# Sliding-window attention feeding a routed MLP: half-width values, in-place keys, 64-row score tiles, chained loads

## The chip, the cores and the metric

The kernel runs on one core of a Trainium2 chip. The time is the device time of one execution in microseconds. The kernel before took 681.13 us (median of 3 runs, 680.95 to 684.59). The profiled execution took 682.57 us; its span from first to last instruction is 680.8 us, at a mean granted TensorE clock of 0.992.

Names of engines: PE is TensorE (PEld its weight loads), DVE is VectorE, ACT is ScalarE, POOL is GpSimd, SP is the sync engine, which here only starts transfers.

## The reference

```python
# attention: 8 batches, 8 heads, 512 local and 32 global rows, head_dim 64
out_g = softmax(q_g @ [k_g, k_l].T / 8) @ [v_g, v_l]           # global rows see everything
s_ll  = where(abs(i - j) <= 32, q_l @ k_l.T / 8, -1e9)         # local rows: a band of +-32
out_l = softmax([q_l @ k_g.T / 8, s_ll]) @ [v_g, v_l]          # ... and the 32 global keys
x     = concat([out_g, out_l], rows), heads side by side       # (8, 544, 512)
# routing: logits = x @ w_gate (8 experts); local = sigmoid(x @ w_local)
# the expert of a row is the argmax of its logits, or the row before's if local >= 0.5
out   = softmax(logits)[e] * (relu(x @ w1[e]) @ w2[e])         # 512 -> 1024 -> 512, fp32
```

## The kernel before, in words

Two stages follow each other. **Attention** fills the first 228 us or so; the routed MLP ("MoE") fills the rest. The change lies in attention and in the hand-over of buffers to the MoE.

*Tiling of attention.* Two heads make a pair, so a batch has four pairs; a pair's 64 + 64 head dimensions fill the 128 partitions. The 512 local rows are 16 windows of 32 rows. A window needs 128 keys: its own 32, the 32 on each side, and the 32 global ones; so its scores are one 128-wide block.

- `load` and `loadv` start a pair's transfers on the SP queue: q and k into a `raw` buffer (528 KB, four buffers) and v into a `v` buffer (1040 KB, four buffers). v comes from memory already arranged as the 128 value rows of every one of the 16 windows, so each value row is stored about twice and the global ones 16 times.
- `prep` (GpSimd) builds from `raw` what the scores read: `qbd`, a block-diagonal q (head 0's 64 dimensions in partitions 0 to 63, head 1's below, zeros elsewhere, written once by `blank`), and `kx`, the keys with the global 32 between the local ones, so that any window's 128 keys are contiguous. `cp` does this with GpSimd's affine_select.
- `l_m` writes the band mask into two PSUM banks with a matmul of the identity. `l_s` adds the scores: one matmul a window with 128 contraction rows, 64 output columns (2 heads by 32 queries) and 128 keys; two windows stand side by side in a bank.
- `l_max` (DVE) takes the row maximum and subtracts it, `l_exp` (ACT) exponentiates, `l_t` (PE, then ACT) transposes, `l_av` multiplies by v: 128 rows, 32 columns, 65 wide (a column of ones gives the sum); then DVE divides into `xa`, the batch's rows.
- The global queries of two pairs make a unit "g" (`g_s`, `g_max`, `g_exp`, `g_t`, `g_av`), which reads k in `raw` and six of the 16 window arrangements of v (`GCH`).

*Order.* Everything is written out by hand in `run`: 48 steps, of a batch l0, l1, g0, l2, g1, l3 (l = a pair, g = the global queries of two). Step s does scores, maximum and exponent of unit s and transposes and values of unit s - 2. Engines execute their queues in the order in which `run` writes them. In between stand pieces of later work: `fpiece(wide)` and `fpiece(thin)` (f1 transposes finished rows, f2 and f3 compute gate logits), and `drip`, which puts one or a few small DVE or GpSimd instructions of the routing (`gens`) between others. `moe.pre` starts, in the last four steps, the first gathers of MoE rows (`gather`, GpSimd), the first weight loads, and splits of weights into high and low parts (`split`, `flush`; two of them with the subtraction on GpSimd). `f4` stores a finished batch's rows: one transfer of 1056 KB on the ACT queue (SP for the last two batches) and small ones for the global rows.

*PSUM.* Scores of l and g units and some routing pieces share three banks (`ps0` to `ps2`); a unit takes two, so a unit's second bank is one that the unit before last, or the one before, must have released: DVE's subtraction releases a bank.

Lines of the profile: L246 scores, L235 mask, L263 transposes of l units, L279 values, L331/L342 the same of g units, L299 global scores, L355 f1, L370 f2, L190 GpSimd copies, L251/L253 maximum and subtraction, L282 to L287 division, L307 maximum of g units, L1284/L1296 the MoE's matmuls, L1191 the low part of weights, L1224 gathers.

## Time and profile before

| | busy us of 680.8 | in 123.00 to 149.20 (one batch in the middle of attention) |
|---|---|---|
| PE | 651.2 | 25.84 |
| PEld | 560.6 | 21.31 |
| DVE | 430.1 | 21.31 |
| ACT | 344.6 | 16.07 |
| POOL | 205.8 | 11.03 |
| DMA engines, mean share | | 0.86 (299 GB/s) |
| profiled execution / its span | 682.57 / 680.8 us | |
| median of the runs | 681.13 us | |

A batch repeats every 26.2 to 26.3 us there. Busy time of PE counts matmuls as pipelined, with modelled ends; rows of one line that overlap the next line's are shown with their own length, while the chain of waits shows what each adds.

### The profile page before, as it was taken

What the parts mean: (1) busy time and instruction counts of PE and PEld (TensorE: products, weight loads), DVE (VectorE), ACT (ScalarE), POOL (GpSimd) and SP (SyncE); (2) the same over time, 40 slices, a digit from 0 to 9 for tenths busy, and PEclk for the clock granted to TensorE, in tenths of its full rate; (3) what the DMA queues carried; (4) which work ended last, traced back from release to release, by engine and by line L of the source; (5) the groups of instructions that cost most, each with busy time, mean ns of one, the idle gap of its engine ahead of it and who ended that gap; (6) DMA issues with size and microseconds to landing.
All of it is one profiled execution on the core that took longest, in us unless ns stands there. A gap on an engine that the chain in (4) does not pass through costs nothing.

```text
span 680.8 us, 18547 instructions
## 1 busy us (share of the span) xinstructions
PE 651.2 (96%) x7261; PEld 560.6 (82%) x7261; DVE 430.1 (63%) x1090; ACT 344.6 (51%) x620; POOL 205.8 (30%) x342
## 2 busy tenths in 40 slices
PE   8899999998999999999999999999999999999994
PEld 6688788786776879887889888889898989898893
DVE  7878687787987877976407545526363627265552
ACT  4465665664555764555317626334455326166543
POOL 7644344343662310033012313040304020133113
PEclk9999999999999999989999999999999999999997
DMA  8857978879585596867318566437374626175583
GB/s 321 350 202 265 322 253 333 306 260 345 206 317 201 194 344 214 294 199 235 117 41 293 201 252 201 148 101 272 88 274 139 218 67 243 54 277 185 182 288 99
DMA packets 43013, 151.46 MB, mean 222 GB/s; under 512 B 7965, under 2 KB 9245, under 8 KB 38688
## 3 DMA queue, kind: packets, MB, share of 16 engines
q1 hardware_dynamic: 32080, 120.42, 50.5%
q0 software_dynamic: 6960, 21.90, 9.8%
q10 hardware_dynamic: 3744, 6.63, 2.6%
q8 instruction: 78, 1.28, 0.8%
q14 instruction: 151, 1.24, 0.6%
HBM read 130.55 MB, written 19.69 MB: 221 GB/s over the span
## 4 chain that ended last, share of the span: by engine, by line
PE 81%; DVE 10%; issue 4%; POOL 2%; ACT 1%; DMA 1%; POOLq 0%; ACTq 0%; DVEq 0%
PE ps L1284 27%; PE ps L1296 23%; PE ps L246 7%; PE ps L263 4%; PE ps L279 4%; PE ps L1238 3%; PE ps L1301 2%; PE ps L355 2%; DVE wp L1191 2%; PE ps L342 2%; PE ps L299 2%; PE ps L331 2%; PE ps L370 1%; DVE pe L253 1%; DVE mx L251 1%
## 5 line engine op out<-in xcount | busy, mean ns | idle before, releaser
L1312 POOL DMA_INDIRECT out_dram<-y,tk x39 | 41.3, 1058 | 311.8 <-ACT y L1309 155.4
L1284 PE MATMUL ps<-wp,wp 128*128 128x256 f32 (+6 forms) x744 | 118.0, 318 | 0.0
L1284 PEld LDWEIGHTS ps<-wp,wp 128*128 128x128 f32 x744 | 112.0, 189 | 5.4 <-ACT wp L1240 0.4
L1296 PE MATMUL ps<-wp,wq 128*128 128x512 f32 x444 | 111.5, 398 | 0.5 <-DVE wq L1288 0.5
L1296 PEld LDWEIGHTS ps<-wp,wq 128*128 128x128 f32 x444 | 81.6, 188 | 17.8 <-ACT wq L1286 0.7
L1288 DVE SCALAR_TENSOR_TENSOR wq<-ps,wq 128x384 fp32r<-128x384 f32 (+4 forms) x120 | 44.9, 409 | 55.9 <-ACT wq L1286 49.8
L1286 ACT ACTIVATE wq<-ps 128x256 fp32r<-128x256 f32 (+6 forms) x88 | 39.4, 452 | 72.7 <-PE ps L1284 65.8
L190 POOL TENSOR_SCALAR_AFFINE_SELECT qbd<-raw 64x512 f32<-64x512 f32 x62 | 44.3, 715 | 97.3 <-PE ps L246 89.0
L1241 DVE TENSOR_TENSOR wp<-ps,wp 128x512 fp32r<-128x512 f32 x40 | 27.6, 691 | 71.5 <-ACT wp L1240 71.3
L246 PE MATMUL ps<-kx,qbd 128*64 128x128 f32 x1024 | 64.7, 276 | 3.7 <-issue 3.6
L246 PEld LDWEIGHTS ps<-kx,qbd 128*64 128x64 f32 x1024 | 55.4, 137 | 11.7 <-issue 9.1
L251 DVE TENSOR_REDUCE mx<-ps 128x4 f32<-128x512 f32 x64 | 43.8, 685 | 30.0 <-PE ps L246 28.8
L1309 ACT ACTIVATE y<-ps,pp 128x512 f32<-128x512 f32 x39 | 26.8, 687 | 66.4 <-PE ps L1296 60.2
L257 ACT ACTIVATE pe<-pe 128x512 f32<-128x512 f32 x64 | 40.8, 638 | 37.9 <-DVE pe L253 37.9
L1191 DVE TENSOR_TENSOR wp<-raw,wp 128x1024 fp32r<-128x1024 f32 x47 | 56.7, 1218 | 4.5 <-ACT wp L1178 4.3
L1224 POOL DMA_INDIRECT xa<-xs,idx x42 | 50.5, 1203 | 17.3 <-issue 11.1
L1240 ACT CAST wp<-ps 128x512 fp32r<-128x512 f32 x40 | 23.3, 586 | 55.5 <-PE ps L1238 55.5
L1178 ACT CAST wp<-raw 128x1024 fp32r<-128x1024 f32 x49 | 50.6, 1047 | 0.9 <-PE ps L342 0.6
L253 DVE TENSOR_TENSOR pe<-ps,mx 128x512 f32<-128x512 f32 x64 | 43.9, 686 | 1.0
L190 POOL TENSOR_SCALAR_AFFINE_SELECT kx<-raw 128x384 f32<-128x384 f32 (+3 forms) x127 | 42.8, 370 | 2.7 <-DMA raw<-in_qk_dram 0.6
L279 PEld LDWEIGHTS ps<-v,pt 128*32 128x32 f32 x2048 | 32.1, 110 | 11.4 <-issue 8.8
L265 ACT COPY pt<-ps 128x512 f32<-128x512 f32 x64 | 34.7, 599 | 10.8 <-PE ps L263 10.8
(284 smaller groups left out, 1183.0 us busy)
## 6 DMA issues: line engine op xcount, KB each, us to landing
raw<-in_w_dram SPq DMA_DIRECT2D x78, 512.0 KB
v<-in_vw_dram SPq DMA_DIRECT2D x32, 1040.0 KB
raw<-in_qk_dram SPq DMA_DIRECT2D x32, 528.0 KB
xa<-in_w_dram SPq DMA_DIRECT2D x26, 512.0 KB
xT<-in_w_dram SPq DMA_DIRECT2D x20, 512.0 KB
xs<-xa ACTq DMA_DIRECT2D x6, 1056.0 KB
xs<-xa SPq DMA_DIRECT2D x2, 1056.0 KB
qgb<-in_qg_dram SPq DMA_DIRECT2D x8, 128.0 KB
```

The source lines that it names most:

```text
L190: self.nc.gpsimd.affine_select(out=out, in_=in_, pattern=pat, compare_op=ALU.is_ge, fill=0.0, base=0, channel_multiplier=0)
L246: nc.tensor.matmul(sp[64 * t2:64 * t2 + 64, t], qbd[:, w], kf[:, f:f + P], start=False, stop=True, skip_group_check=True)
L251: nc.vector.tensor_reduce(out=mx, in_=st["sps"][hb], axis=AX.X, op=ALU.max)
L253: nc.vector.tensor_tensor(out=st["pe"][:, 4 * hb:4 * hb + 4], in0=st["sps"][hb], in1=mx.broadcast_to([P, 4, P]), op=ALU.subtract)
L279: nc.tensor.matmul(o[32 * w4:32 * w4 + 32, g, h], pt[:, 2 * g + w4 // 2, w4 % 2, h, :], v[:, w, h * (D + 1):(h + 1) * (D + 1)], start=True ...
L1178: (nc.vector.tensor_copy if dve else nc.scalar.copy)(out=hi, in_=raw)
L1191: (nc.gpsimd if pool else nc.vector).tensor_tensor(out=lo[:, f], in0=raw[:, f], in1=hi[:, f].bitcast(F32), op=ALU.subtract)
L1224: self.nc.gpsimd.indirect_dma_start(out=self.xr[j] if k == "early" else self.xr4[:, j], out_offset=None, in_=src, in_offset=bass.IndirectO ...
L1284: nc.tensor.matmul(ph, a[:, dc, fs], b_[:, dc, n0:n1], start=(n == 0), stop=(n == 11))
L1288: nc.vector.scalar_tensor_tensor(out=t, in0=ph[:, a - n0:b_ - n0], scalar=0.0, in1=hh[:, fc, a:b_].bitcast(F32), op0=ALU.max, op1=ALU.subt ...
L1296: nc.tensor.matmul(py, a[:, fc, js], b_[:, fs], start=(fc == 0 and k == 0), stop=(fc == 7 and k == 2))
L1312: sc = nc.gpsimd.indirect_dma_start(out=self.out, out_offset=bass.IndirectOffsetOnAxis(ap=self.g[1][:, j:j + 1], axis=0), in_=y, in_offset ...
```

## The change

1. **v by halves.** Only the 128 value rows of the eight even windows are loaded (520 KB a pair). `prepv` lets GpSimd build the odd windows' rows in a second tile `w` (three buffers): one copy of 96 partitions by 1040 elements and one of 32 partitions by 910 that moves from partitions 0-31 to 96-127. The even windows read `v`, the odd ones `w`.
2. **Keys in place.** `kx` is gone. `raw` is 2064 wide instead of 1056; the loaded keys stand in pairs of 64 in the order `PO`, and `prep` writes, with two copies of 448 elements, 14 blocks of 64 (global keys, a neighbour's keys) behind them in the same buffer. A window's 128 keys are now two blocks of 64 at two places (`keys`).
3. **Narrow scores.** Pairs 0 and 2 of each batch (`NARROW`) have no `qbd`: `l_sn` issues 32 matmuls of 64 contraction rows by 32 columns, one for each window and head, head 0 into one bank and head 1 into the other; then come both maxima. Pairs 1 and 3 keep `l_s`. The mask is written by two matmuls a bank, each half as wide, in place of one.
4. **Chain of loads.** `get` makes each q/k or v load, from the fourth, wait until the last but one load before it has landed.
5. **Row stores.** A batch's rows leave as two halves on the SP queue, at most one half a step; the small store `gx` goes to SP too.
6. **Order.** `fpiece(thin)` (f2, f3) moves from ahead of the exponent to between the two `l_av` (or behind `g_av`); `g_exp` has three activations in place of five, with the global scores split at 320 instead of 256; `blank` and the mask stand differently at the start.
7. **Space.** The gathered rows `xr`, the MoE's output tiles `y` and one weight buffer now lie in the wider `raw` buffers.

```diff
-GCH = [1, 4, 7, 10, 13, 14]
+GCH = [8, 2, 11, 5, 14, 0]
+PO = [0, 2, 3, 5, 6, 1, 4, 7]
+AHEAD, FREE = 2, 3
+NARROW = (0, 2)
...
+    def get(self, out, in_):
+        d = self.nc.sync.dma_start(out, in_)
+        if len(self.sent) >= FREE:
+            self.tc.add_manual_dep(d.ins, self.sent[-AHEAD].ins.name, ..., reason="chain")
+        self.sent.append(d)
...
+        if not u["n"]:
+            qbd = u["qbd"] = self.qbd()
             self.cp(qbd[0:64, :, 0, :], q[0:64], [[0, NW], [0, 32]])
             self.cp(qbd[64:128, :, 1, :], q[64:128], [[0, NW], [0, 32]])
-        self.cp(kf[:, 1:5]...); self.cp(kf[:, 6:24]...); self.cp(kf[:, 24]...); self.cp(kx[:, 1:8, 2, :]...)
+            self.cp(x[:, :, 0], g, [[0, 14], [0, 32]])
+            self.cp(x[:, :, 1], k[:, 1:15], [[0, 14], [0, 32]])
...
+    def prepv(self, u):
+        w = self.w()
+        self.cur[b]["v"][pr] = (v, w)
+        self.cp(w[0:96], v[0:96], [[0, 8], [0, VW]])
+        self.cp(w[96:128, 0:7], v[0:32, 1:8], [[0, 7], [0, VW]])
...
+    def l_sn(self, st):
+        for t2 in range(2):
+            for par in range(2):
+                for w4 in range(4):
+                    m = 4 * t2 + w4
+                    w = 2 * m + par
+                    k = self.keys(st, m, par)
+                    for h in range(2):
+                        d = slice(64 * h, 64 * h + 64)
+                        nc.tensor.matmul(st["sps"][h][32 * w4:32 * w4 + 32, 2 * par + t2],
+                                         st["qk"][d, 32 * w:32 * w + 32], k[d], start=False, stop=True, ...)
...
                 if npr < len(pairs):
                     self.prep(pairs[npr])
+                self.prepv(nx)
+            self.store(1)
...
-            if nl:
+            if nl and nx["n"]:
+                self.l_sn(nx)
+                self.l_max(nx, 0)
+                self.l_max(nx, 1)
+            elif nl:
                 self.l_s(nx, 0)
                 self.l_max(nx, 0)
...
-            fpiece(thin)
             if nl:
                 self.l_exp(nx, 0)
             ...
             if sl:
                 self.l_av(st, 0)
+                fpiece(thin)
                 self.l_av(st, 1)
...
-        self.xr = [buf.tile([P, ROW], F32, name=f"xr{j}") for j in range(2)]
+        self.xr = [raw.t[j][:, 1024:1024 + ROW] for j in range(2)]
```

How the rows move is shown at three places.

On PE, in step l2 of the first batch, before (L235 writes the mask, L246 the scores, L279 the values):

```order
L263 MATMUL ps_68<-idf,pe_138 128x128 x4
L235 LDWEIGHTS idb
L235 MATMUL ps_63<-mask,idb 128x4x2x32
L235 LDWEIGHTS idb
L235 MATMUL ps_64<-mask,idb 128x4x2x32
L246 MATMUL ps_63<-kx_146,qbd_144 64x128 x8
L246 MATMUL ps_64<-kx_146,qbd_144 64x128 x8
L279 MATMUL ps_70<-v_134,pt_142 32x65 x16
```

and the same place after (L258 mask, L284 the narrow scores, of which the first three of 32 are shown):

```order
L302 MATMUL ps_68<-idf,pe_139 128x128 x4
L258 LDWEIGHTS idb
L258 MATMUL ps_63<-maskn,idb 128x4x32
L258 LDWEIGHTS idb
L258 MATMUL ps_63<-maskn,idb 128x2x2x32
L258 LDWEIGHTS idb
L258 MATMUL ps_64<-maskn,idb 128x4x32
L258 LDWEIGHTS idb
L258 MATMUL ps_64<-maskn,idb 128x2x2x32
L284 MATMUL ps_63<-raw_79 32x128
L284 MATMUL ps_64<-raw_79 32x128
L284 MATMUL ps_63<-raw_79 32x128
```

Sixteen matmuls of 64 columns, eight for one bank and then eight for the other, became 32 of 32 columns that alternate between the banks; the mask has four matmuls and weight loads in place of two.

On DVE, at the start of the program, from the mask to the first row maximum, before:

```order
L146 CAST mask<-m_155 128x512
L147 MEMSET mask 64x32
L148 MEMSET mask 64x32
L202 COPY qbd_144<-raw_77 64x16x32
L203 COPY kx_146<-raw_77 128x7x32
L217 MEMSET qbd_145 64x16x32
L218 MEMSET qbd_145 64x16x32
L219 MEMSET kx_147 128x32
L220 MEMSET kx_147 128x64
L455 MEMSET pg_149 128x768
L251 TENSOR_REDUCE mx_119<-ps_63 128x4
```

and after (`maskn` is the narrow pairs' mask; L157 waits for two GpSimd copies that read it):

```order
L153 CAST maskn<-m_155 128x2x32 x2
L154 CAST maskn<-m_155 128x128
L157 MEMSET maskn 32x32
L158 MEMSET maskn 32x32
L159 MEMSET mask 64x32
L160 MEMSET mask 64x32
L225 COPY raw_77<-raw_77 128x14x32
L500 MEMSET pg_148 128x768
L241 MEMSET qbd_145 64x16x32
L242 MEMSET qbd_145 64x16x32
L241 MEMSET qbd_146 64x16x32
L242 MEMSET qbd_146 64x16x32
```

All four large `qbd` memsets now stand between the first pair's keys and the first maximum; before, two of them stood there and two ahead of the mask.

On POOL, at the end of attention (L1224 and L1191 before, L1280 and L1247 after, are the MoE's first gathers and splits), before:

```order
L1224 DMA xr_86<-xs,idx 128x528
L1224 DMA xr_87<-xs,idx 128x528
L190 AFFINE_SELECT qbd_145<-raw_80 64x16x32 x2
L190 AFFINE_SELECT kx_147<-raw_80 128x128
L190 AFFINE_SELECT kx_147<-raw_80 128x6x64
L190 AFFINE_SELECT kx_147<-raw_80 128x32
L190 AFFINE_SELECT kx_147<-raw_80 128x7x32
L1224 DMA xr_86<-xs,idx 128x528
L1224 DMA xr_87<-xs,idx 128x528
L1191 TENSOR_TENSOR wp_100<-raw_77,wp_100 128x256 x4
L1191 TENSOR_TENSOR wp_101<-raw_78,wp_101 128x256 x4
```

and after:

```order
L1280 DMA raw_77<-xs,idx 128x528
L1280 DMA raw_78<-xs,idx 128x528
L208 AFFINE_SELECT qbd_146<-raw_80 64x16x32 x2
L208 AFFINE_SELECT raw_80<-raw_80 128x14x32 x2
L208 AFFINE_SELECT w_135<-v_133 96x1040
L208 AFFINE_SELECT w_135<-v_133 32x910
L1280 DMA raw_77<-xs,idx 128x528
L1280 DMA raw_78<-xs,idx 128x528
L1247 TENSOR_TENSOR wp_98<-raw_77,wp_98 128x256 x4
L208 AFFINE_SELECT w_136<-v_134 96x1040
L208 AFFINE_SELECT w_136<-v_134 32x910
L1247 TENSOR_TENSOR wp_99<-raw_78,wp_99 128x256 x4
```

The last pair's `w` now stands between the two splits, and the first gathers write into `raw` buffers that global scores still read.

More of the change, by code (lines that the diff above doesn't have):

```diff
@@ L131, in __init__ @@
         self.pq = []
+        self.sent = []
+        self.rows = []
         self.gens = []
@@ L233, in l_m, with keys @@
         for hb, sp in enumerate(st["sps"]):
[L234 to L235 removed]
+            so = sp.rearrange("p t (k c) -> p t k c", c=32)
+            for par, mo in enumerate((so[:, 0:2, 1::2, :], so[:, 2:4, 0::3, :])):
+                nc.tensor.matmul(mo, self.cst.idb, self.maskn[:, par] if st["n"] else self.mask[:, hb, par], start=(par == 0), stop=False, skip_group_check=True)
+    def keys(self, st, m, par):
+        far = min(max(2 * m - 1, 1), 14) if par == 0 else min(2 * m + 2, 14)
+        u0, u1 = 8 + PO.index(m), 16 + 2 * PO.index(far // 2) + far % 2
+        return st["qk"][:, 0:2048].rearrange("p (u c) -> p u c", c=64)[:, u0:u1 + 1:u1 - u0]
     def l_s(self, st, hb):
         nc = self.nc
[L239 to L240 removed]
         sp = st["sps"][hb]
```

136 lines of the change are left out of this document (73 added, 63 removed).

## The prediction

> **What bounds the kernel now.** I read the page first, for who is on the chain that ended last:
>
> ```profile
> span 680.8 us, 18547 instructions
> PE 81%; DVE 10%; issue 4%; POOL 2%; ACT 1%; DMA 1%; POOLq 0%; ACTq 0%; DVEq 0%
> PE ps L1284 27%; PE ps L1296 23%; PE ps L246 7%; PE ps L263 4%; PE ps L279 4%; PE ps L1238 3%; PE ps L1301 2%; PE ps L355 2%; DVE wp L1191 2%; PE ps L342 2%; PE ps L299 2%; PE ps L331 2%; PE ps L370 1%; DVE pe L253 1%; DVE mx L251 1%
> ```
>
> PE carries 81% of the chain, and the scores L246, which the change rebuilds, are 7% of it, about 50 us. DMA is 1%. Next the engines' busy time by stretches of attention (columns: length, PE, PEld, DVE, ACT, POOL, clock, DMA share, GB/s):
>
> ```profile
> 96.70:123.00 26.30, 25.95 (x590) 21.49 (x591) 21.04 (x73) 16.07 (x38) 11.05 (x24) 1.00 0.85 298
> 180.00:211.00 31.00, 28.64 (x619) 23.05 (x618) 27.04 (x102) 17.16 (x44) 22.11 (x41) 1.00 0.79 283
> ```
>
> In the middle PE is busy 25.95 of 26.30 us, DVE 21.04, POOL 11.05: a batch takes what its matmuls take. From 180 us, where the routing joins in, DVE (27.04 of 31) comes close to PE (28.64). So shorter matmuls shorten attention until DVE's 21 us a batch, or POOL, stands in the way. Transfers, busy as they are (0.85), release almost nothing on the chain.
>
> **A, narrow scores.** PE's timeline of a step l0 shows what one pair costs; the pieces of the chain give what each adds:
>
> ```profile
> 134.54 0.88 PE L331 MATMUL ps<-idf,pg 128*128 128x128 f32 x6
> 135.26 0.38 PE L235 MATMUL ps<-mask,idb 128*128 128x256 bf16 x2
> 135.47 0.60 PE L355 MATMUL ps<-idf,xa 128*128 128x128 f32 x4
> 136.00 1.97 PE L246 MATMUL ps<-kx,qbd 128*64 128x128 f32 x32
> 137.90 0.89 PE L342 MATMUL ps<-v,ptg 128*32 128x65 f32 x48
> 158.21 0.22 PE ps L235 x2
> 158.87 1.90 PE ps L246 x32
> 160.76 1.05 PE ps L279 x64
> ```
>
> A matmul here is two records. L246 has two column tiles: 32 records in 1.90 us, so a tile is held 1.90 x 2 / 32 = 0.119 us by one. L279 has four: 64 records in 1.05 us, one every 16 ns, each holding its tile 1.05 x 4 / 64 = 0.066 us for 65 columns; scaled to 128 that is 0.129, near 0.119, so column tiles do run side by side. Eight tiles of 64 rows by 32 columns appear nowhere. If all eight overlap, 64 records need 64 x 0.119 / 8 = 0.95 us; at the pace of L279, 1.05; if the two row halves exclude each other, 64 x 0.119 / 4 = 1.90, no gain. Slower than 1.90 would need fewer than four tiles at once, which L279 excludes. I take 1.05, since the record count and the column width of the stationary operand are L279's: **16 pairs x (1.05 - 1.90) = -13.6 us**, bounds -15.2 and 0.
>
> [...]
>
> **B, masks.** Four half-wide matmuls stream what two did (0.22 us), with two more weight loads. The row nearest to a loaded 128-column bf16 stationary is routing's:
>
> ```profile
> 201.76 0.93 PE L1023 MATMUL ps<-oe,o 128*128 128x12 bf16 x21
> ```
>
> 21 loads and matmuls in 0.93 us, 44 ns each, less than the 55 ns that a half-wide mask streams; so they may hide. Bounds 0 and 32 x 2 x 0.044 = 2.8; I take **+1.0**.
>
> **C, start.** PE waits for DVE at the start, on a bank that DVE's first subtraction releases:
>
> ```profile
> 3.64 0.21 POOL L144 TENSOR_SCALAR_AFFINE_SELECT m<-m 32x32 f32<-32x32 f32 x1
> 5.10 0.52 DVE L203 COPY kx<-raw 128x224 f32<-128x224 f32 x1
> 5.67 0.48 DVE L217 MEMSET qbd<- 64x512 f32 x1
> 6.30 0.48 DVE L218 MEMSET qbd<- 64x512 f32 x1
> 7.10 0.70 DVE L455 MEMSET pg<- 128x768 f32 x1
> 7.72 0.63 DVE L251 TENSOR_REDUCE mx<-ps 128x4 f32<-128x512 f32 x1
> 9.12 0.27 PE L235 MATMUL ps<-mask,idb 128*128 128x256 bf16 x1 [1.40 <-DVE pe L253]
> ```
>
> After: the mask's source is ready at 3.85 (3.64 + 0.21); three small casts to about 4.3; two GpSimd copies of 256 (the 224-element copy below takes 0.42) to about 5.2; four small memsets to 5.6; the key copy of 448, its 224 being 0.52, to 6.35; pg 0.70; four memsets 0.58 apart (5.67 to 6.30, less the gap) to 9.35. The first maximum moves from 7.72 to 9.35: **+1.6**; with GpSimd copies between 0.3 and 1.2 us each, +1.3 to +3.1.
>
> **D, what DVE and POOL do to the gain.** A batch's PE work falls by 1.7 to about 24.5, still above DVE's 21.0. GpSimd's copies cost, by form:
>
> ```profile
> L190 POOL TENSOR_SCALAR_AFFINE_SELECT qbd<-raw 64x512 f32<-64x512 f32 x62 | 44.3, 715 | 97.3 <-PE ps L246 89.0 <-DMA raw<-in_qk_dram 4.1 <-DMA xr<-xs,idx 2.1
> L190 POOL TENSOR_SCALAR_AFFINE_SELECT kx<-raw 128x384 f32<-128x384 f32 x32 | 17.8, 555 | 0.0
> L190 POOL TENSOR_SCALAR_AFFINE_SELECT kx<-raw 128x224 f32<-128x224 f32 x31 | 12.9, 416 | 0.0
> L190 POOL TENSOR_SCALAR_AFFINE_SELECT kx<-raw 128x128 f32<-128x128 f32 x32 | 9.5, 295 | 2.7 <-DMA raw<-in_qk_dram 0.6
> ```
>
> From 128 to 384 elements the time rises by 0.26 us, 1.02 ns an element: 448 take 0.62, 1040 take 1.22, 910 take 1.09. So `w` is 2.3 us a pair, the in-place keys 1.25, and a batch on POOL is 2 x 2 x 0.72 + 4 x 1.25 + 4 x 2.3 = 17 us of 24.5, up from 11. It fits: each copy is issued two steps ahead of its reader, and POOL now idles 89 us waiting for L246. In 180 to 211, 22.1 + about 7 nearly fills 31 - 2; there the key copies stand ahead of `w` and routing's tiles, and have slack:
>
> ```profile
> L921 POOL TENSOR_SCALAR o<-io,plo 128x128 bf16<-128x128 bf16 x15 | 8.9, 606 | 3.5 <-DVE plo L904 3.5
> ```
>
> But two costs stay. DVE's wait ahead of a step is short:
>
> ```profile
> 132.73 0.69 DVE L251 TENSOR_REDUCE mx<-ps 128x4 f32<-128x512 f32 x1 [1.83 <-PE ps L246]
> 142.02 0.69 DVE L251 TENSOR_REDUCE mx<-ps 128x4 f32<-128x512 f32 x1 [1.20 <-PE ps L246]
> ```
>
> Between these, steps l3 and l0 keep DVE busy without a pause. With l0 0.85 shorter, DVE is late by some 0.3 when l1's mask wants a bank: 0.3 x 6 = 1.8 us. The chain runs through DVE from its first row here to its last:
>
> ```profile
> 173.03 0.18 DVE ei L853
> 190.24 0.21 DVE leq L742
> ```
>
> so the one narrow step in it gains nothing: 0.85. And small DVE operations between SBUF tiles are stretched in places, as shortest, median and longest of one line show (ns):
>
> ```profile
> L772 DVE TENSOR_SCALAR lsu<-lsu x8: 160/338/496, 60.3 to 262.8; 128x5 f32<-128x5 f32 x8
> ```
>
> If POOL does that, its busier 17 us add to it. [...] Some 14 such operations a batch, 0.18 (median less shortest) each, a quarter more often: 0.6 a batch, of which I count 1.35 us where DVE leads. **D = 1.8 + 0.85 + 1.35 = +4.0**; bounds +1 (only what hides nowhere) and +8 (DVE gives back over half of A).
>
> **E, transfers.** Of v, half of 32 x 1040 KB goes, and at most two loads are in flight. DMA ends almost no step of the chain, so the transfers themselves gain 0. PE does stand still for "issue":
>
> ```profile
> v<-in_vw_dram SPq DMA_DIRECT2D x32, 1040.0 KB
> ...
> PE ps L246 <- issue: 3.6, 2, 2.0
> PE ps L342 <- issue: 2.2, 3, 1.5
> PE ps L279 <- issue: 1.5, 4, 0.5
> ```
>
> Of these 7.3 us the profile doesn't say what PE waits for; if it is instructions fetched behind bulk transfers, quieter queues help, while 12% more PE records in attention (16 x 32 + 64 on some 8 x 591) hurt. **-1.5**; bounds -5 and +0.5. Row stores in halves ride on SP behind loads that wait anyway, and `xa` has three buffers: 0. Fewer activations in `g_exp` and f2 behind the exponent relieve ACT (16 of 26 us): 0, covered by PE.
>
> **F, hand-over.** The second split feeds an MoE matmul closely:
>
> ```profile
> 227.67 2.83 POOL L1191 TENSOR_TENSOR wp<-raw,wp 128x256 fp32r<-128x256 f32 x4 [0.97 <-ACT wp L1178]
> 230.44 1.21 PE L1284 MATMUL ps<-xh,wp 128*128 128x256 f32 x8
> 203.38 1.18 POOL L1224 DMA_INDIRECT xr<-xs,idx  x1 [0.93 <-DVE idx L1026]
> 207.66 1.14 PE L299 MATMUL ps<-raw,qgb 128*64 128x256 f32 x8
> 215.33 0.66 PE L1238 MATMUL ps<-idf,xr 128*128 128x128 f32 x4
> ```
>
> The split ends at 230.50 and its readers start half way through 230.44 to 231.65. `w`'s 2.3 us ahead of it fill its 0.97 wait and push it 1.3 later, against 0.4 of slack: **+1.0**, bounds 0 and +2.3. The first gather now waits for L299's end (208.8, not 203.4) and holds `prep` behind it; its rows are read at 215.3 and the last pair's keys later still: 0. `y` and weights in `raw` overlap in no columns: 0.
>
> **Sum.** -13.6 + 1.0 + 1.6 + 4.0 - 1.5 + 1.0 = -7.5. Profiled: 682.6 - 7.5 = 675.1. The median of the runs shown lies 1.4 below the profiled run: 681.1 - 7.5 = **673.6**. Its own range, terms varied in turn: 667 to 679.
>
> **Rivals.** (1) *The row halves take turns*, or starts have a floor above L279's 16 ns (L1023's are 44 ns apart). From the middle, 1.48 us a narrow step, to 1.90, A is -6.8 to 0 and D +2.5 to +1; the sum is -2.2 to +3.1: 679 to 684. For it: no such tile in the trace; against: how well L279's four tiles overlap. [...] (2) *DVE takes PE's place*: D = +8, sum -3.5, 677.6. For it: 27.04 of 31 late in attention; against: 21 of 24.5 elsewhere. (3) *GpSimd becomes the bound, the slower side*: the copy of `w` moves partitions, which no row shows. Once a pair's `w` takes (24.5 - 7.9) / 4 = 4.1 us, POOL sets the batch; at 4.6 it is 26.3 a batch, all of A is lost, the last two batches with 9 us of routing add about 5, with C, F and E 6 more than before: 687. Against: forms of 64 and 128 partitions cost alike. (4) The halved transfer was hidden anyway: that is in the forecast already, as E.
>
> **Chances.** Forecast 0.64, (2) 0.14, (1) 0.10, (3) 0.10, anything else slower 0.02. What can be told from no change is 0.5%, 3.4 us: faster is under 677.7, slower over 684.5. Faster: 0.62 + 0.08 + 0.02 = 0.72; same: 0.02 + 0.06 + 0.08 = 0.16; slower 0.12. The range takes in the forecast's bounds and (1) and (2): 664 to 683.
>
> **What would show it.** A: 64 records of L284 in about 1.05 us. B: L258 at 0.22 to 0.31 a pair. C: first maximum near 9.3. D: a batch of 24.5 to 25, DVE's waits ahead of maxima gone, POOL near 17. E: "issue" under 7. F: PE waiting for POOL in the first expert. Wrong: L284 near 1.9, PE waiting for `w`, or new waits in the MoE, where I expect none.

## The result, and the profile after

| | before | after |
|---|---|---|
| median of the runs | 681.04 us (4 runs, 680.09 to 684.59) | 692.69 us (4 runs, 689.96 to 693.23) |
| profiled execution / its span | 682.57 / 680.8 us | 693.23 / 691.5 us |
| ratio after / before | | 1.0149, 95% interval 1.0117 to 1.0182 |

The change makes the kernel about 1.5% slower; the forecast was 673.6 us (664 to 683), faster. It missed both the side and the range. Ratios, here and below, compare executions in the chip's faster state alone, while medians are over all.

The page of the changed kernel, span and chain that ended last:

```profile
span 691.5 us, 19682 instructions
PE 73%; DVE 17%; issue 5%; ACT 2%; POOL 1%; POOLq 0%; DVEq 0%; ACTq 0%
PE ps L1340 24%; PE ps L1352 23%; PE ps L322 4%; PE ps L302 3%; PE ps L271 3%; PE ps L1294 3%; DVE mx L290 2%; DVE pe L292 2%; PE ps L1357 2%; PE ps L284 2%; DVE wp L1247 2%; PE ps L394 2%; PE ps L341 2%; PE ps L381 1%; PE ps L370 1%
```

PE's share of the chain fell from 81 to 73%, DVE's rose from 10 to 17%. (L322 is now the values, L284 the narrow and L271 the wide scores, L290 and L292 maximum and subtraction, L258 the mask, L208 GpSimd's copies.) Where that happens is read from one stretch of each trace, from the first score to the last value product of attention; first before, then after (columns: length, PE, PEld, DVE, ACT, POOL, clock, DMA share, GB/s):

```profile
5.21:237.20 231.99, 218.79 (x4776) 179.91 (x4776) 187.56 (x641) 133.63 (x303) 108.41 (x242) 1.00 0.78 279
```

```profile
6.32:246.10 239.78, 211.79 (x5350) 171.57 (x5350) 195.50 (x640) 128.13 (x271) 150.56 (x212) 0.99 0.62 197
```

The 10.7 us between the spans are 1.1 at the start (the first score at 6.32, not 5.21), 7.8 in this stretch, and 1.8 behind it. In the stretch PE has 7.0 us *less* to do, and stands still for 28.0 us instead of 13.2. DVE does the same number of instructions (640 and 641) and needs 7.9 us longer for them. PE's two longest waits for DVE in this stretch before (in all, times, longest):

```profile
PE ps L235 <- DVE pe L253: 1.6, 2, 1.4
PE ps L235 <- DVE leq L742: 0.8, 1, 0.8
```

and its longest waits of any kind after:

```profile
PE ps L258 <- DVE pe L292: 4.5, 2, 2.8
PE ps L322 <- issue: 3.9, 4, 1.4
PE ps L381 <- DVE rs L324: 3.1, 2, 2.3
PE ps L381 <- issue: 3.1, 2, 2.8
PE ps L284 <- issue: 3.0, 5, 1.0
PE ps L322 <- ACT pe L296: 2.3, 4, 0.9
PE ps L394 <- issue: 2.0, 2, 1.4
PE ps L322 <- DVE xg L388: 1.5, 1, 1.5
```

Three things are to be seen: waits for DVE, which were 3.2 us in all before and are 12.0 now; "issue" (PE stands still and the profile shows nothing that it waits for), 9.2 before and 12.8 now; and 2.3 for exponents of ACT, which in turn read what DVE's subtraction leaves. DVE has not become the engine that all others wait for, though: ahead of its maxima it still waits 30.0 us for scores, as it did before (first row before, second after).

```profile
L251 DVE TENSOR_REDUCE mx<-ps 128x4 f32<-128x512 f32 x64 | 43.8, 685 | 30.0 <-PE ps L246 28.8
L290 DVE TENSOR_REDUCE mx<-ps 128x4 f32<-128x512 f32 x64 | 43.8, 684 | 30.0 <-PE ps L271 15.2
```

The chain shows the first kind at work. From the third batch, in order of time (start, length, what):

```profile
91.41 0.60 DVE mx L290
92.01 0.49 DVE lsu L827
92.50 0.57 DVE pe L292
93.07 0.60 DVE mx L290
...
94.72 0.94 DVE gx L833
95.66 0.02 issue
95.68 0.42 DVE xa L329
96.10 0.07 DVE rs L324
96.17 0.55 DVE xa L836
...
97.30 0.24 PE ps L322
```

`gx` is 32 x 8 elements and holds the chain for 0.94 us; `xa` of L836 is 128 x 4 elements and holds it for 0.55. Together these two small operations between SBUF tiles cost twice a maximum of 128 x 512 (0.68). Shortest, median and longest of `gx` (ns), before and after:

```profile
L778 DVE TENSOR_TENSOR gx<-lpr,lsu x8: 156/354/659, 64.2 to 264.4; 32x8 f32<-32x8 f32 x8
```

```profile
L833 DVE TENSOR_TENSOR gx<-lpr,lsu x8: 122/534/924, 67.3 to 273.2; 32x8 f32<-32x8 f32 x8
```

What stretches them can be seen in the changed kernel's trace. Of its eight `gx`, five take 496 to 924 ns; each of the five started while a GpSimd instruction ran, and each ended within 22 ns of that instruction's end. The other three (122, 148 and 163 ns) started with GpSimd idle. The reciprocal of the division, also between SBUF tiles but with one input, has not changed (median 178 ns in both traces): 29 of its 64 started during one of GpSimd's copies (L208), and none took more than 179 ns.

### The profile page after: what moved, and what is told of

The parts are those of the page before. It is cut to its first block, busy times and chain, and to the rows that moved or that the text cites. A ratio compares the mean times of both kernels' runs of the same rounds, so it can differ in the third digit from the quotient of the medians.

```text
span 691.5 us, 19682 instructions
## 1 busy us (share of the span) xinstructions
PE 645.0 (93%) x7837; PEld 552.1 (80%) x7837; DVE 438.3 (63%) x1092; ACT 338.8 (49%) x588; POOL 248.9 (36%) x313
## 4 chain that ended last, share of the span: by engine, by line
PE 73%; DVE 17%; issue 5%; ACT 2%; POOL 1%; POOLq 0%; DVEq 0%; ACTq 0%
PE ps L1340 24%; PE ps L1352 23%; PE ps L322 4%; PE ps L302 3%; PE ps L271 3%; PE ps L1294 3%; DVE mx L290 2%; DVE pe L292 2%; PE ps L1357 2%; PE ps L284 2%; DVE wp L1247 2%; PE ps L394 2%; PE ps L341 2%; PE ps L381 1%; PE ps L370 1%
## 5 line engine op out<-in xcount | busy, mean ns | idle before, releaser
L1368 POOL DMA_INDIRECT out_dram<-raw,tk x39 | 40.3, 1033 | 313.2 <-ACT raw L1365 153.6
L1340 PE MATMUL ps<-wp,wp 128*128 128x256 f32 (+6 forms) x744 | 118.1, 318 | 0.0
L1340 PEld LDWEIGHTS ps<-wp,wp 128*128 128x128 f32 x744 | 111.8, 189 | 5.6 <-ACT wp L1296 0.4
L208 POOL TENSOR_SCALAR_AFFINE_SELECT w<-v 96x1040 f32<-96x1040 f32 x64 | 67.1, 1048 | 39.0 <-PE ps L381 32.7
L290 DVE TENSOR_REDUCE mx<-ps 128x4 f32<-128x512 f32 x64 | 43.8, 684 | 30.0 <-PE ps L271 15.2
L1365 ACT ACTIVATE raw<-ps,pp 128x512 f32<-128x512 f32 x39 | 26.8, 688 | 67.7 <-PE ps L1352 60.6
L1247 DVE TENSOR_TENSOR wp<-raw,wp 128x1024 fp32r<-128x1024 f32 x47 | 56.8, 1219 | 4.5 <-ACT wp L1234 4.2
L1280 POOL DMA_INDIRECT xa<-xs,idx x42 | 52.1, 1240 | 16.8 <-issue 10.2
L208 POOL TENSOR_SCALAR_AFFINE_SELECT raw<-raw 128x448 f32<-128x448 f32 x62 | 38.9, 653 | 20.1 <-DMA raw<-in_qk_dram 18.9
L322 PEld LDWEIGHTS ps<-v,pt 128*32 128x32 f32 x1024 | 32.4, 109 | 16.1 <-issue 7.4
L322 PE MATMUL ps<-v,pt 128*32 128x65 f32 x1024 | 39.9, 222 | 5.2 <-ACT pe L296 2.3
L292 DVE TENSOR_TENSOR pe<-ps,mx 128x512 f32<-128x512 f32 x64 | 43.9, 686 | 0.8
L322 PE MATMUL ps<-w,pt 128*32 128x65 f32 x1024 | 40.1, 222 | 3.4 <-issue 3.4
```

Of the source, the lines that this page charges most:

```text
L208: self.nc.gpsimd.affine_select(out=out, in_=in_, pattern=pat, compare_op=ALU.is_ge, fill=0.0, base=0, channel_multiplier=0)
L290: nc.vector.tensor_reduce(out=mx, in_=st["sps"][hb], axis=AX.X, op=ALU.max)
L292: nc.vector.tensor_tensor(out=st["pe"][:, 4 * hb:4 * hb + 4], in0=st["sps"][hb], in1=mx.broadcast_to([P, 4, P]), op=ALU.subtract)
L322: nc.tensor.matmul(o[32 * w4:32 * w4 + 32, g, h], pt, v[par][:, m, h * (D + 1):(h + 1) * (D + 1)], start=True, stop=True, skip_group_check ...
L1247: (nc.gpsimd if pool else nc.vector).tensor_tensor(out=lo[:, f], in0=raw[:, f], in1=hi[:, f].bitcast(F32), op=ALU.subtract)
L1280: self.nc.gpsimd.indirect_dma_start(out=self.xr[j] if k == "early" else self.xr4[:, j], out_offset=None, in_=src, in_offset=bass.IndirectO ...
```

## The experiments

**Theories.** (1) GpSimd's new long copies hold up DVE's small operations, DVE is late with its banks, PE waits; 1a says that such an operation waits for the end of the copy that it meets, 1b that the two share a bandwidth. (2) The narrow steps make DVE late by themselves, since both maxima stand behind all 32 matmuls. (3) f2 and f3 in their new place make PE wait. (4) The chain of loads holds back work that needs q and k. (5) PE's program arrives late where its instructions are dense (formed after the first runs). All runs, each ratio against the kernel before timed beside it, with its 95% interval. The median of that kernel lay between 677.9 and 681.0 us beside different runs, so comparisons across groups go by the ratios:

| run | what | median us | ratio to before | interval |
|---|---|---|---|---|
| (the change) | | 692.7 | 1.0149 | 1.0117 to 1.0182 |
| e4 | before + two idle GpSimd copies a pair | 688.8 | 1.0139 | 1.0091 to 1.0187 |
| e10 | change, no copies into w | 683.5 | 1.0115 | 1.0066 to 1.0163 |
| e13 | change, copies in pieces | 684.1 | 1.0043 | 1.0020 to 1.0066 |
| e2 | change, no narrow pair | 686.1 | 1.0091 | 1.0057 to 1.0125 |
| e14 | change, four narrow pairs | 690.0 | 1.0132 | 1.0095 to 1.0170 |
| e11 | no copies, no narrow pair | 680.9 | 1.0059 | 1.0016 to 1.0102 |
| e9 | no narrow pair, idle PE instructions | 690.0 | 1.0165 | 1.0116 to 1.0215 |
| e1 | w loaded from memory, chain kept | 704.0 | 1.0369 | 1.0293 to 1.0446 |
| e5 | change without the chain | 700.8 | 1.0309 | 1.0248 to 1.0371 |
| e6 | w loaded, no chain | 704.8 | 1.0380 | 1.0315 to 1.0445 |
| e7 | w loaded, no chain, idle copies | 718.7 | 1.0469 | 1.0374 to 1.0564 |
| e8 | w loaded, no chain, no narrow pair | 683.8 | 1.0043 | 0.9985 to 1.0101 |
| e3 | f2 and f3 in their old place | 694.6 | 1.0228 | 1.0179 to 1.0277 |
| e12 | all blanks behind step 0's maxima | 695.5 | 1.0254 | 1.0194 to 1.0315 |
| e15 | one blank ahead, one behind | 691.6 | 1.0155 | 1.0120 to 1.0189 |
| e16 | wide, half of the copies, start of e15 | 685.6 | 1.0067 | 1.0043 to 1.0092 |
| e17 | pieces, start of e15 | 684.2 | 1.0107 | 1.0062 to 1.0153 |
| e18 | pieces, start of e15, wide | 687.5 | 1.0136 | 1.0106 to 1.0166 |

### GpSimd's copies: e4, e10, e13

e4 puts the copies alone into the kernel before:

```diff
                 if npr < len(pairs):
                     self.prep(pairs[npr])
+                v = self.cur[nx["u"][0]]["v"][nx["u"][1]]
+                self.cp(self.junk[0:96], v[0:96, 0:8], [[0, 8], [0, VW]])
+                self.cp(self.junk[96:128, 0:7], v[0:32, 1:8], [[0, 7], [0, VW]])
```

> The kernel before, and in each step of a pair two more GpSimd copies of the size of those that fill w (96 x 1040 and 32 x 910 elements), from v into a tile that nothing reads in attention. Nothing waits for their result. Theory 1: small DVE operations between SBUF tiles are stretched, maxima come late and the kernel slows by 4 to 11 us, to 685 to 692. Theory 2: GpSimd has room (11 of 26 us a batch), within 1.5 us of before.

Measured 1.0139. Nothing waits for these copies' result, yet attention grows from 231.99 to 241.83 us and DVE's busy time from 187.56 to 195.62, by as much as in the changed kernel:

```profile
5.47:247.30 241.83, 222.37 (x4777) 182.29 (x4776) 195.62 (x641) 133.45 (x303) 173.95 (x306) 0.99 0.75 267
```

Theory 1 gave 4 to 11 us, the ratio says 9.5; theory 2 by itself had under 1.5. But the path is for the most part not the one that theory 1 names. The copies also delay GpSimd's own work behind them: `o`, tiles of the routing that PE multiplies (L1027). PE waits 4.4 us for them, which it did not before, and at the end of the longest of these waits, from 210.11, the granted clock is at 0.5 for 6.83 us, 3.4 us lost:

```profile
PE ps L1027 <- POOL o L925: 4.4, 3, 3.6
200.00:220.00 20.00, 15.02 (x301) 12.33 (x298) 11.44 (x40) 7.89 (x18) 16.20 (x26) 0.83 0.62 213
```

That is 7.8 of the 9.8 us by which attention grew in this profile, while PE's waits for DVE grew from 3.2 to 5.6. So e4 shows that the copies stretch DVE's operations and cost 1.4% in all; it does not show that DVE's delay is what costs it. In the changed kernel PE waits only 0.5 us for GpSimd in this stretch, so there this second path plays hardly a part.

e10 takes them out of the changed kernel (odd windows read `v` itself):

```diff
-        w = self.w()
-        self.cur[b]["v"][pr] = (v, w)
-        self.cp(w[0:96], ...); self.cp(w[96:128, 0:7], ...)
+        self.cur[b]["v"][pr] = (v, v)
```

> The changed kernel without GpSimd's copies into w: the odd windows read the even windows' tile v instead, so a quarter of their value rows are the wrong ones (left out: the copy, 2.1 us of GpSimd a pair). Narrow scores, half transfers and chain stay. Theory 1 alone: DVE's waits on PE fall from 12 to 5 us or less and the time to 680 to 685. Theory 5: PE then reaches the ends of its program blocks sooner, 'issue' rises from 12.8 to 20 us or more, the clock falls to half after long stalls, and little is gained: 689 to 697.

```profile
6.31:233.80 227.49, 209.53 (x5350) 170.97 (x5350) 184.93 (x640) 127.48 (x271) 84.22 (x148) 0.98 0.64 208
```

In the profile, which is of the fastest of the four runs, DVE's time falls by 10.6 us (195.50 to 184.93) and attention by 12.3. DVE's share of the chain that ended last falls from 17 to 13%:

```profile
PE 78%; DVE 13%; issue 4%; POOL 1%; ACT 1%; DMA 1%; POOLq 0%; DVEq 0%; ACTq 0%
```

PE's waits for DVE fall to 9.0 us only, where theory 1 had 5 or less; "issue" did not rise as theory 5 said but fell, to 8.3. The median, 683.5, lies in theory 1's range, but the kernel before, timed beside it, was 2.7 us faster than beside the change, and the ratio (1.0115) overlaps the change's 1.0149. So this run does not settle the size of the gain; the next one does better, and tells how the two engines meet:

```diff
-        self.cp(w[0:96], v[0:96], [[0, 8], [0, VW]])
-        self.cp(w[96:128, 0:7], v[0:32, 1:8], [[0, 7], [0, VW]])
+        for k in range(0, 8, 2):
+            self.cp(w[0:96, k:k + 2], v[0:96, k:k + 2], [[0, 2], [0, VW]])
+        for k in range(0, 7, 2):
+            n = min(2, 7 - k)
+            self.cp(w[96:128, k:k + n], v[0:32, k + 1:k + 1 + n], [[0, n], [0, VW]])
```

> The changed kernel with w copied in eight pieces of two windows (260 elements, about 0.3 us each) in place of two copies of 1.05 us. Theory 1a (a small DVE operation that meets a GpSimd copy waits for its end): the longest of the small DVE operations fall from about 1.0 us to 0.4 and the time by 3 to 6 us, to 687 to 690. Theory 1b (both share the bandwidth for as long as the copies run in all): the same stretched total, 691 to 695.

1.0043, where the change has 1.0149; the intervals are well apart, and the difference is some 7 us, more than the 3 to 6 that theory 1a had. The pieces move the same bytes and keep GpSimd busy *longer* in attention (175.64 us, not 150.56), since a piece of 260 elements takes 0.41 us, not a quarter of 1.05 (the second row is the changed kernel's, the others are e13's, where `gx` is L836):

```profile
6.32:238.00 231.68, 210.65 (x5350) 170.99 (x5351) 188.38 (x640) 128.09 (x271) 175.64 (x404) 0.99 0.64 202
L208 POOL TENSOR_SCALAR_AFFINE_SELECT w<-v 96x1040 f32<-96x1040 f32 x64 | 67.1, 1048 | 39.0 <-PE ps L381 32.7
L208 POOL TENSOR_SCALAR_AFFINE_SELECT w<-v 96x260 f32<-96x260 f32 x128 | 48.0, 409 | 21.9 <-PE ps L384 21.6 <-PE ps L397 0.2
L836 DVE TENSOR_TENSOR gx<-lpr,lsu x8: 124/192/573, 64.7 to 265.0; 32x8 f32<-32x8 f32 x8
```

The median `gx` is down from 534 to 192 ns, DVE's busy time by 7.1 us. A shared bandwidth (1b) would have made DVE wait at least as long; what counts is the length of one GpSimd instruction (1a), as the ends of `gx` above show too. The copy `xa` (L836 of the changed kernel) has one input and is stretched too: the five of its eight that started while a GpSimd instruction ran took 188 to 1074 ns, and each ended 25 to 30 ns behind that instruction's end; the other three took 153 to 172. The reciprocal has one input as well and keeps its time, so the number of inputs does not tell which operations wait. What does was not shown.

How DVE's time becomes PE's is less plain. Of PE's standstill in attention (28.0 us in the change, 21.0 in e13), waits for DVE went only from 12.0 to 11.2 us; "issue" went from 12.8 to 7.1 and waits for ACT from 2.6 to 0.8. That shorter copies save the kernel time is shown; why it appears as less "issue" is open.

### The narrow scores: e2, e14, e11, e9

e2 is the change with `NARROW = ()`.

> All four pairs of a batch keep the wide scores; GpSimd's copies of v and all else as changed (qbd is built for every pair, two more GpSimd copies of 0.7 us for each of 16 pairs). Theory 1: the stretched DVE operations remain and DVE sets the pace, so little changes: 690 to 696. Theory 2: the time falls to 683 to 687, the narrow steps being the cause.

```profile
8.42:240.20 231.78, 220.60 (x4838) 184.41 (x4838) 195.43 (x637) 128.40 (x271) 170.03 (x240) 0.99 0.63 200
```

Without narrow pairs PE has 8.8 us more to do (220.60 and 211.79), and in these profiles attention is 8.0 us *shorter* (231.78 and 239.78). DVE's 195.4 us are the same, so the copies' cost is in both. "issue" of PE is 0.1 us in place of 12.8, waits for DVE 7.9 in place of 12.0. The median, 686.1, is what theory 2 said and too fast for theory 1 alone: the narrow pairs seem to cost something of their own, although the intervals (up to 1.0125, from 1.0117) just touch. e14, `NARROW = (0, 1, 2, 3)`:

> All four pairs of a batch narrow. My forecast of the narrow scores by themselves: another -13.6 us of PE work, less what DVE gives back, so 684 to 692. Theory 5 (program blocks): PE's 'issue' in attention goes from 12.8 to 20 us or more, and the time to 696 to 706.

Measured 690.0, 1.0132: theory 5's time (696 to 706) is missed, though "issue" did rise to some 20 us in the profile, which is of the slowest run (698.1 us); the median lies where the forecast of the scores allowed it, but the ratio is not to be told from the change's own. No, two or four narrow pairs cost 1.0091, 1.0149 and 1.0132: the time does not follow PE's work. The forecast's 13.6 us for two pairs would be a step of 0.020 down between neighbours; none is there. e11 repeats the comparison without the copies (e10 with `NARROW = ()`):

> The same without GpSimd's copies into w, and with wide scores for all pairs: neither of the two causes is there, half transfers and chain stay. Theories 1 and 5 together: DVE's waits at about 3 to 4 us and 'issue' under 3 us; 673 to 679, faster than before. If the chain or the half transfers cost something by themselves: 680 to 686.

```profile
8.42:232.90 224.48, 217.73 (x4838) 182.71 (x4838) 185.76 (x637) 128.08 (x271) 104.26 (x176) 0.99 0.64 208
```

The time missed (680.9, 1.0059; 673 to 679 expected): attention is 7.5 us shorter than before the change, but it starts 3.2 us later (first score at 8.42, behind GpSimd's `qbd`), and the rest of the kernel took 2.3 longer. The comparison stands: PE does 8.2 us more than in e10, and attention is 3.0 shorter. So the narrow scores gain nothing that can be told even without the copies; PE's waits for DVE are 9.0 us with them (3.3 of it the wait at the start) and 3.5 without, "issue" 8.3 and 2.4. How much of the 5.7 and 3.5 is theory 2, the order of the maxima, and how much just a shorter step was not taken apart.

e9 tells what "issue" has to do with it: wide scores, and 32 idle one-column PE matmuls more in the value step of pairs 0 and 2.

```diff
...
+        if pr in (0, 2):
+            for k in range(16):
+                r = 32 * (k % 4)
+                nc.tensor.matmul(ob[r:r + 32, 300:301], self.cst.idb[:, 0:32], self.cst.idb[:, 0:1], start=True, stop=True, ...)
```

> The changed kernel with wide scores for all pairs, and in the value step of pairs 0 and 2 of each batch 32 more tiny PE matmuls (identity, one column, into columns of the bank that nothing reads): as many PE instructions more as the narrow scores bring, without their geometry and without their order of maxima. Their own time at the pace of the value matmuls is 32 x 16 ns x 16 pairs = 8 us. Theory 5 (PE's program arrives in blocks of 127 matmuls; denser PE instructions use a block up before the next has come, and PE stands still for 'issue'): 'issue' of PE in attention, which is 0.1 us with wide scores, goes to 6 us or more, with gaps at multiples of 127 matmuls. Theory 2 (it is the order of the maxima): 'issue' stays under 2 us.

```profile
PE ps L327 <- issue: 2.4, 1, 2.4
...
PE ps L271 <- issue: 1.7, 2, 1.0
PE ps L346 <- issue: 1.4, 1, 1.4
```

"issue" goes from 0.1 to 6.2 us (5.5 in the rows shown), with no narrow tile and the maxima in their old order, as theory 5 said. Waits for DVE rise too, from 7.9 to 10.0 us. Where it falls is worked out from the trace's records, as the number of the matmul record, counted from the first, before which PE stood still for "issue" for over 0.3 us:

```
after  349  603  857  984  1619  1874  2255  2891  3272  3526  4289  4925
e6     349  603  984  1239  1620  1874  2001  2255  2891  3273  3527  3908  4289  4544  4798  4925
e9     1873  2509  3145  3653  4034
```

The distances are multiples of 127, to a record or two: 254, 254, 127, 635, 255, 381, 636 and so on. In the kernel before, six of nine such places stand at the same count (222, 349, 476, 1491, 3270, 3397) and hold 7.0 of its 9.2 us of "issue". A matmul record comes with one weight load (7837 of each in the changed kernel), so 127 of them are 254 instructions, and in the trace's DMA queue 8, of the kind "instruction", packets of 16,384 bytes follow each other at that pace: 42 began by 246.1 us, and PE came to 42 such counts in that time (by the author's estimate, 16,384 / 254, about 64 bytes an instruction). Before record 349 of the changed kernel the packet ran from 21.10 to 22.18 us, PE stood from 22.24 and went on at 23.62: 1.4 us behind the landing; at the other waits of over 0.6 us for "issue" in this trace it went on 1.3 to 1.7 us behind one. Counts and landings together point to PE waiting there for the next block of its own program; no row of the profile names that wait. The blocks are used up fastest where matmuls are small: narrow scores and value products are issued at 16 to 17 ns a matmul, and the fastest block of 127 in attention is gone in 3.2 us (3.9 before the change; the median is 5.4, and was 6.0). What starts such a packet, and so how early it could come, no run here shows.

### Transfers and chain: e1, e5, e6, e7, e8

e1 loads `w` from memory where GpSimd copied it (the input holds its rows behind those of `v`; this load is not part of the chain):

```diff
...
-        self.cp(w[0:96], ...); self.cp(w[96:128, 0:7], ...)
+        self.nc.sync.dma_start(w.rearrange("p w c -> p (w c)"), self.vw[b, pr, :, 8 * VW:])
```

> The odd windows' tile w is loaded from memory, 520 KB a pair, as a second transfer in the place where GpSimd copied it; GpSimd does no copies of v. All else is as changed. Theory 1 (GpSimd's long copies hold up DVE's small operations between SBUF tiles, DVE falls behind and PE waits for its banks): most of the 11 us by which attention grew, and some of the gain of the narrow scores, come back: 674 to 682 us; the small DVE groups (gx, leq, xa<-tok) return to the mean times of before (310, 194, 212 ns). Theory 2 (the narrow steps' order, both maxima behind all 32 matmuls, makes DVE late by itself): 689 to 693. Theory 4 (the chain of loads holds back the work that needs q and k): 692 to 697, since twice as many bytes of v go again.

1.0369, slower than any theory had it. GpSimd waited 52.6 us for q and k ahead of the in-place keys. The reading then was that with 520 KB a pair more, two loads at a time are too few, and that the run tested the chain. e5 (`FREE = 1000`, no chain), e6 (e1 and e5), e7 (e6 and two idle copies a pair) and e8 (e6 with `NARROW = ()`) take it away:

> The changed kernel without the chain: a load of q/k or v waits only for its buffer. Theory 4 (the chain delays q and k; GpSimd waits 18.9 us for raw, and with it the in-place keys and w): 684 to 689 us. If the chain is harmless (theory 1 alone, DVE held up by GpSimd's copies): 691 to 694.

> w loaded from memory (520 KB a pair more), GpSimd copies no v, and no chain; narrow scores, in-place keys, order as changed. In the run with w loaded and the chain kept, GpSimd waited 52.6 us for q and k, so that run tested the chain, not GpSimd. Theory 1 (GpSimd's copies hold up DVE): 673 to 681, attention shorter than before. Theory 2 (the narrow steps make DVE late by themselves): 684 to 690.

> As the run with w loaded and no chain, and GpSimd makes the two copies of v of each pair into a tile that nothing reads in attention. The difference to that run is the price of the copies alone. Theory 1: +6 to +12 us. Theory 2: under +2.

> As the run with w loaded and no chain, but with wide scores for all pairs. The difference to that run is the worth of the narrow scores when GpSimd does not copy v. My forecast of the narrow scores (-13.6 on PE, less what DVE gives back, 4): the wide variant 6 to 10 us slower. Theory 2: the wide variant 2 to 6 us faster.

Theory 4 falls: without the chain the changed kernel is slower (1.0309), not faster. e6, expected at 673 to 690, came out at 704.8, and e8, the same with wide scores, at 683.8, level with before. So with full transfers the narrow scores cost some 21 us, where the forecast had them gain. PE's waits in e6 say how:

```profile
PE ps L321 <- issue: 8.4, 6, 3.4
PE ps L380 <- issue: 6.3, 3, 2.5
PE ps L283 <- issue: 5.5, 6, 1.7
...
PE ps L408 <- issue: 3.5, 1, 3.5
PE ps L393 <- issue: 3.0, 1, 3.0
```

30.5 us of "issue" in all, against 4.8 in e8. And long ones cost a second time. Stretches of e6 (length, PE, clock, DMA share, GB/s):

```profile
24.00:28.00 4.00, 1.71 (x8) 0.84 0.65 255
28.00:32.00 4.00, 4.00 (x72) 0.73 0.21 42
32.00:36.00 4.00, 4.00 (x122) 1.00 1.00 372
```

PE waited 3.0 us until 26.29, and from 26.73 the granted clock was 0.5 for 3.41 us, which costs 1.7. In e6's attention half-clock stretches add up to 17 us lost; in the changed kernel there is one, at the start (below), in the kernel before none. The length of the wait alone does not tell when the clock falls: in e6 waits of 2.1 us until 39.38 and of 1.7 until 189.61 had half the clock behind them, from 40.38 and 190.57, while the changed kernel's waits of 2.8 us until 145.1 and 2.3 until 173.0 cost no clock (1.00 in 145 to 149 and in 171 to 175). What else decides it was not shown.

e7 against e6 prices idle copies in this setting at 1.0469 against 1.0380, in the direction of theory 1, but the intervals overlap. e1, with the chain, and e6 without are level (1.0369 and 1.0380), while the change is well ahead of e5: the chain helped only where the loads were halved.

### Order and start: e3, e12, e15

e3 puts `fpiece(thin)` back ahead of the exponent.

> The pieces f2 and f3 stand ahead of the exponent again, as before the change. Theory 3 (f2 and f3 between the two value products make PE wait there): 686 to 690. Theories 1 and 2: 691 to 695.

1.0228: theory 3 is wrong in its sign. With f2 and f3 in their old place the kernel is some 5 us slower, though the intervals just touch (1.0182 and 1.0179); the forecast had 0. That the place itself does this isn't shown: in e3's profile PE waits 5.0 us for `o`, GpSimd's routing tiles, where the changed kernel has no such wait, and the clock is at 0.5 for 6.83 us from 207.14, 3.4 us lost.

e12 and e15 ask for the price of the start. In the changed kernel:

```profile
10.96 0.39 PE L258 MATMUL ps<-mask,idb 128*128 128x128 bf16 x2 [2.81 <-DVE pe L292]
11.28 3.40 PE L271 MATMUL ps<-raw,qbd 128*64 128x128 f32 x32
0.00:18.50 18.50, 13.77 (x207) 0.91 0.71 232
```

The wait of 2.81 us is followed by wide scores that take 3.40 us in place of 1.90, at a clock of 0.91 over these 18.5 us (0.5 from 10.85 to 14.26). e12 moved all blanks behind step 0's maxima:

```diff
         self.prep(pairs[0])
-        nc.vector.memset(self.pg.t[1], 0.0)
-        for k in range(2):
-            self.blank(k)
...
             if s == 0:
+                for k in range(2):
+                    self.blank(k)
+                nc.vector.memset(self.pg.t[1], 0.0)
```

> The changed kernel with the four memsets of qbd and the one of pg behind step 0's maxima (pair 0 is narrow and reads no qbd). Term C: the first maximum moves from 9.48 to about 6.5 us, PE's wait of 2.8 us at 10.96 goes. If that wait is what brings the granted clock to 0.5 between 10.8 and 14.3 us, the clock stays at 1.00 there and 3.0 + 1.7 = 4 to 5 us are gained: 687 to 689. If the clock falls for another reason: 689 to 691.

The first maximum came at 7.50, but step 1's scores then waited for the first `qbd`'s blanks until 11.50, and the clock still fell; 1.0254, a miss. e15 leaves `self.blank(0)` where it was:

> The changed kernel with the memsets of the first qbd where DVE idles ahead of the first maximum, and those of the second qbd and of pg behind step 0's maxima (in the run with all of them behind, step 1's wide scores waited for the first qbd's blanks until 11.5). Theory C: first maximum at 7.5 to 8, step 1's scores from about 9.5 in place of 11.3, no wait over 2 us and so no halved clock at the start: 687 to 690. Otherwise 691 to 694.

```profile
8.12 0.69 DVE L290 TENSOR_REDUCE mx<-ps 128x4 f32<-128x512 f32 x1 [0.74 <-PE ps L284]
9.59 0.28 PE L258 MATMUL ps<-mask,idb 128*128 128x128 bf16 x2 [1.36 <-DVE pe L292]
0.00:18.50 18.50, 13.66 (x236) 1.00 0.72 236
```

Here the start is as expected, and so is the clock (1.00). The time is not: 691.6, 1.0155. In its profile half-speed came later instead, 3.41 us from 171.5, behind a wait for DVE of 2.5 us; most of the start's gain was gone from there on. It may be that, while such waits remain, taking one away only shifts where the clock falls; that isn't shown.

### What is left: e16, e17, e18

e16 makes all pairs but the first wide, lets GpSimd copy only the 96 shared rows of `w`, in pieces, and loads the other 32; e17 is e13 with e15's start, e18 the same with all pairs but the first wide.

> Wide scores for all pairs but the very first, GpSimd copies only the 96 shared rows of w in pieces of two windows, the 32 far rows of w come from memory (116 KB a pair), half transfers of v and chain as changed, and the start of the run before this one. By the differences measured so far: wide 686, half of the copies gone -2 to -3, the start -2 to -4: 679 to 682, no faster than the kernel before. If the pieces also keep DVE from waiting: 675 to 679, faster than both.

> The changed kernel with w in eight pieces and the earlier start, pairs 0 and 2 narrow. If the gain of the start (1.4 us at the first maximum, and the halved clock behind the wait of 3 us) is kept: 680 to 683, level with the kernel before. If stalls of over 2 us for 'issue' elsewhere halve the clock again: 683 to 686.

> The same with wide scores for all pairs but the very first. My forecast of the narrow scores (16 x 0.85 us of PE less what DVE gives back): this one 6 to 10 us slower than with narrow pairs. Theory 5 with theory 1 (standstill for 'issue' and DVE's waits take the gain of narrow scores): within 2 us of it, 680 to 685.

None beats the kernel before; e13 and e8, at 1.0043, come nearest, and e8's interval takes in 1. e16 shows that the single gains do not add up (685.6, expected 675 to 682), and why it comes out no better than e13 is open. e17 and e18 differ in the narrow scores alone: 3.2 us for them, with overlapping intervals (1.0107 and 1.0136); that is half of what the forecast expected there and more than theory 5 did. Pieces and start together (1.0107) are no better than pieces alone (1.0043). Nor is a gain of the pieces to be seen where the scores are wide: e18, with pieces and the earlier start, has 1.0136, and e2, with the long copies, 1.0091. In e18's profile PE waits 4.3 us for GpSimd's `o`, as in e4, and the clock is at 0.5 for 6.83 us from 210.21: with wide scores GpSimd also builds `qbd` for nearly all pairs, and the pieces keep it busy longer. So the gain of the pieces is shown beside narrow pairs only, by e13; between e15 and e17 it is 0.0048, some 3 us, with overlapping intervals.

## Why the prediction was wrong, by its steps

The forecast was -7.5 us; by the ratio the change cost some 10. Two steps carry most of that: D, whose stretched operations were put at 1.35 us where cutting the copies into pieces saves some 7 (e13; some 3, less surely, between e15 and e17), and A, whose 13.6 us did not arrive.

- **A, narrow scores: size of one step right, worth wrong.** The chain's pieces have "1.09 PE ps L284 x64" (1.05 forecast) and 1.90 for a wide step, so the row halves do overlap (with the forecast's 0.119 us a tile, 64 x 0.119 / 1.09 is 7.0 tiles at once) and rival (1) is out, also with its floor for starts: 64 records in 1.09 us are 17 ns apart. But the -13.6 was entered into the sum as time, and of it nothing arrives that can be told from the noise: no, two and four narrow pairs lie within 0.006 of each other (e2, the change, e14; without copies e11, e10), the narrow ones on the slower side, and e17 against e18 has a gain of 3.2 us with overlapping intervals. PE's busy time, too, falls by only 8.8 us (e2 to the change) and 8.2 (e11 to e10). Standstill for "issue", 0.1 us with wide scores and 12.8 with narrow ones, takes part of the gain; how the rest goes to DVE's waits and to the order of the maxima was not taken apart.
- **B, masks.** L258 is 0.22 us a pair on the chain. The lower bound, 0, would have been the better value.
- **C, start: +1.6 forecast, +1.76 measured** at the first maximum (9.48). What the step left out is that PE's wait grew from 1.4 to 2.81 us and brought half the clock behind it: 1.7 us more.
- **D is the step that failed first.** It had +4.0 with bounds 1 and 8. PE's waits for DVE and ACT grew by 11.2 us (3.5 to 14.7). The three parts of it: bank waits 1.8, one narrow step 0.85, stretched operations 1.35. The last was mis-sized. It took the spread of 0.18 us of the old operations and made them "a quarter more often", because GpSimd is busy a quarter longer; but the stretched `gx` and `xa` ran until the GpSimd instruction that they met had ended (924 and 1074 ns at the longest), and `w`'s copies are 1.05 us in the mean, not 0.3 to 0.7. DVE lost 10.6 us to them (e10), not 8 x 0.6 = 4.8. The sum also counted only a share of that, "where DVE leads". Its picture, that DVE costs something only once its waits ahead of the maxima are gone, did not hold: these waits are 30.0 us before and after, and yet DVE's part of the chain rose from 10 to 17%. And it let DVE cost PE by the waits of the old rhythm, 0.3 us; with e10's unhindered DVE the narrow kernel still waits 5.7 us for it behind the start. The price of the copies on GpSimd was nearly right (2.3 us a pair forecast, 2.1 measured).
- **E, "issue": -1.5 forecast (-5 to +0.5), +3.6 measured.** Both of its directions exist and both were too small: the change with wide scores brings "issue" from 9.2 to 0.1 (e2), and narrow scores in two pairs bring it back to 12.8. The count of "12% more PE records" was taken as an average; what the traces point to is how fast one block of 127 records is used up (3.2 us at the fastest, 3.9 before). The 0 for f2 behind the exponent may be wrong too: e3 is some 5 us slower, with the doubt given there.
- **F, hand-over: +1.0 forecast.** Behind attention the kernel took 1.8 us longer, but over all profiles this part lies between 439 and 456 us without a pattern by the hand-over, so F's time cannot be told. Its sign, PE waiting for GpSimd's split in the first expert, is there but small: 0.5 us (L1340), 0.3 before.
- **Batches** took 26.5 to 33.0 us from 42.5 us on (26.2 to 31.0 before), not 24.5 to 25. GpSimd was at 15 to 21 us a batch (17 forecast), and PE did not wait for it: rival (3) is out as told, and that its time, 687, came closest is chance. Rival (2), DVE in PE's place, came nearest in mechanism, with a price of 677.6 that was 15 us short: by PE's waits its +8 for D should have been 11, and it kept the rest of the gains.

## What to carry to other kernels

Before GpSimd is given a copy because it has time, look at what VectorE does meanwhile: here small operations between SBUF tiles (`gx`, `xa`, not the reciprocal) lasted until the copy had ended, up to 924 and 1074 ns, and with pieces of 0.41 us the median `gx` fell from 534 to 192 ns. So try short instructions, and price the copy by the length of one instruction and not by GpSimd's share. Look also at what GpSimd itself has to deliver behind the copy (e4, e18). Shorter matmuls in a step need not be worth what they take off PE: here it had 8.8 us less to do with two narrow pairs than with none, and no gain could be told from the noise. A run with none and with twice as many shows it in one comparison. Where "issue" sits at multiples of one distance in PE's instruction count (127 matmul records here), ask whether the program is late: 32 tiny matmuls more a step took it from 0.1 to 6.2 us (e9).
